# A gated mix of two long convolutions: B's results multiplied by u as they leave PSUM, two holds copied whole, and a new order

## The chip, the cores and the metric

The kernel runs on one core of a Trainium2 chip. Its engines are called PE (TensorE), DVE (VectorE), ACT (ScalarE), POOL (GpSimd) and SP (SyncE). The metric is the device time of one execution in microseconds. The times of before are three runs.

## The reference

For an input u of 2048 steps by 448 channels, two long convolutions along the steps are computed and mixed by a gate:

```python
x = A_u
g = sigmoid((x * gate_w).sum(-1, keepdims=True))
a = A_ref(x, ...)                  # K[d,l] = Re sum_n C * exp(dt*A*l) * dt*B over 256 modes; y = conv(K, u) + u * Dskip
b = B_ref(x, B_k, B_v, ...)        # kv = shift(k) * v over 4 taps; y = conv(ssm_k, kv) + kv * ssm_D; b = x * y
return g * a + (1 - g) * b
```

So B's convolution result is multiplied by u (`q * y` with q = u), and that product is one of the two operands of the gate. Both convolutions are causal and as long as the sequence.

## The kernel before

The 448 channels are four groups of 112. A tile has 128 partitions, made of 4 channel groups times 32 positions, and 64 blocks of 28 channels in its free dimension. The 112 channels of a group are worked on in four heads H of 28 (NC = 28).

A convolution (`conv_B`, `conv_A`) has these steps for each head. `spread_in` is a first short transform by matmuls with Wc and copies to SBUF (`spread`). `transform` is a second one with the table W2, 64 matmuls and eight copies of 128x896. `swapped` makes a copy with the halves of the partitions exchanged, by eight DMAs on SP's or POOL's queue. `products` are two wide multiplications on DVE. `stage_a` transforms back with copies of up to 128x512, and `stage_b` (heads worked on alone) or `stage_b_both` (B of one head and A of the head before, together) ends it. A's kernel is built beforehand by `table(H)`: exponentials and sines on ACT, then `tables`, a chain of products and additions on DVE (three of them with an accumulating DMA on POOL's queue, `split`), then `sums`, 448 small matmuls on PE, and `gather`.

PSUM is four rooms of two banks (`ps0` to `ps3`, `Places.room`); SBUF scratch is eight slots (`q0` to `q7`). The last part of head 3 is `end`, which also stores the rows to HBM over the queues of SP and ACT; `mix(H)` joins a and b for heads 0 to 2.

`PLAN` (line 37) gives the logical order of the work: T is a table, B and b are B's convolutions, a and A are A's, m is a mix. Nothing is issued in this order. Every engine call is recorded in a list (`Listed`, line 120), and `Order.issue` (line 140) issues the calls in the order written out in the string `ORDER` (line 51), with a dependency that keeps each engine to it. All instructions therefore have one line in the profile, 145. Three more strings fix what could be chosen: `SLOTS` (line 38) and `ROOMS` (line 41) give the buffer of each use, and `SIDES` (line 45) says for each call of a `Sides` helper (line 346: `evac`, `evac.turned`, `evac.ahead`, `evac.minus`, `evac.masked`, `evac.queue`) whether it goes to DVE ("V") or ACT ("S"); for `queue` the two letters are POOL's and SP's DMA queue.

The change touches two places. In `Modes.run` (line 718) the real and imaginary parts of A are copied from PSUM into the tiles that hold them for the tables: one for head 0, one for head 1, one for heads 2 and 3, and each in two halves. In `epilogue_B` (line 948) B's results are copied from PSUM to `ug[H]`, the head's part of the tile natv; after the last block of the head one wide DVE product multiplies all 64 blocks by u (`uu`, the tile natu). Head 0 comes through `stage_b` in two rooms of 32 blocks; heads 1, 2 and 3 come through `stage_b_both` in four rooms of 16 blocks each, with A's results of the head before in the same rooms:

```python
        both = pt[:, :, 0:448].rearrange("p h (b t c) -> p h b t c", t=2, c=NC)
        for t in range(2):
            consume[t](b0, 16, both[:, :, :, t])
```

A's side of a room (t = 1) is read by `gated`, a DVE product with the gate. `less(H)` is the term with which PE subtracts the finished `ug[H]` from A's sums.

Of the kernel before, what the change touches and what calls it, by code (L numbers as in the profile page):

```python
# [10 lines left out]
ALU = mybir.AluOpType  # L11
# [27 lines left out]
    "60254113451327565066707216435622473722641555230367571061240"  # L39
)  # L40
ROOMS = (
    "303201320132221133023000100332000020101102013331223132233010132231223133020313021221212111021000320232120101311331120231"
    "31230230312202203230211002013123100022133320222302200321202302202333012331301212103331312131332201202032310"
)
SIDES = (
    "SSSSVVSVVVVSVVSVVVVVVVVVSVVVSSVVVSSSSSVSVVSSVVSVVSVSSVVSVVVVVVVSSSSSSSSSSSSSSSSSVVVSVSSSVSSSSSSSSSSSSSSSSVSSSSVSVSSSSSSS"
    "SSSSSSSSSSSSSVSSVSSSSSSSSSSVSSSSSSSSSSSSSSSSSSVVSVSSSSSSSSSSSSSSSSSVVVVVVVVVSVVSVVVSSSSSSVSSSSSSSSSSSSVVSVSSSSSSSSSSVSVV"
    "SSSSSSSSSSSVSSSVVSSSSSSSSSSSVSSSSVVVVVVVVSVVVVSVVVSSSVSVVSSSSSSSSSSVVVSVVSSSSSSSSSSSSSSVSSSSSVSSSSSSVSSVSVSSVSSSSVSVVSSS"
    "VSSSSVSSVVVVSSSSSSSSSSVVVSSSSVSSSSVSSSVVSS"
)  # L50
ORDER = (
# [650 lines left out]
class Modes:  # L702
# [15 lines left out]
    def run(self):  # L718
        nc, V, evac = self.nc, self.nc.vector, self.evac
        for c, nm in enumerate(("A_re", "A_im")):  # L720
            pt = self.stepped(nm)
            for h0, h1, t in self.hold:
                for f in range(2):
                    evac(t[:, :, c].rearrange("p h (q w) -> p q h w", w=NC)[:, 4 * f:4 * f + 4],
                         pt[:, f, 0:448].rearrange("p (g h w) -> p g h w", g=4, w=NC)[:, :, h0:h1])
# [401 lines left out]
```

## Time and profile before

| what | us |
|---|---|
| median of three runs (lowest, highest) | 249.13 (248.91, 250.43) |
| profiled execution: time | 247.59 |
| profiled execution: span | 245.7 |
| DVE busy, in 399 instructions | 231.3 |
| ACT busy, in 335 | 219.0 |
| PE busy, in 5451 matmuls | 209.4 |
| POOL busy, in 109 | 37.5 |

The profile is of one execution. The span runs from its first instruction to its end; the execution's own time is 1.9 us longer. Busy time counts each instant of an engine once, while the mean of a group is the full duration of one instruction; neighbours overlap a little. In a row of a group, what follows the first bar is busy time and mean in ns, and after the second bar stands the idle time of the engine just before it and what ended it.

### The profile page before, as it was taken

Reading aid. Unit: us, or ns where it says so; the run is one execution under the profiler, and the core shown is the slowest. Engines: PE = TensorE matmul, PEld = TensorE weight load, DVE = VectorE, ACT = ScalarE, POOL = GpSimd, SP = SyncE. Lnnn points to the kernel's source line nnn. Section 1 sums busy time; section 2 is a strip of 40 time slices with the busy share of each in tenths; the row PEclk is TensorE's granted clock in tenths of the full one; section 3 lists DMA queues with packets and bytes.
Section 4 is the critical chain, followed back from the end, with each engine's and each line's share of the span. In section 5 each row is a group of like instructions: output and inputs, shape, how many; then the busy total and the mean of one; then the engine's idle time right before and its main releaser. Section 6 shows DMA issues by size and latency. Waiting matters only on the chain.

```text
span 245.7 us, 12199 instructions
## 1 busy us (share of the span) xinstructions
PE 209.4 (85%) x5451; PEld 185.2 (75%) x5451; DVE 231.3 (94%) x399; ACT 219.0 (89%) x335; POOL 37.5 (15%) x109
## 2 busy tenths in 40 slices
PE   1557688888989999888999977999999999999970
PEld 1445256766979899788998866889999998998850
DVE  6999999999888999999999999999999999999980
ACT  3897999989999999999999999999999998657820
POOL 8600003040000014000002320000134220300000
PEclk9999799999999999999999999999999999999996
DMA  6999599999002189300476593000248720230046
GB/s 140 311 191 147 123 190 229 188 204 167 7 5 64 39 197 205 93 4 5 78 114 122 104 226 100 7 3 5 39 80 152 187 80 5 63 95 3 3 105 197
DMA packets 43443, 26.27 MB, mean 107 GB/s; under 512 B 34144, under 2 KB 40400, under 8 KB 43392
## 3 DMA queue, kind: packets, MB, share of 16 engines
q1 hardware_dynamic: 39088, 15.98, 30.6%
q0 software_dynamic: 3456, 8.60, 17.6%
q10 hardware_dynamic: 848, 0.92, 1.3%
q8 instruction: 42, 0.69, 1.1%
q14 instruction: 9, 0.07, 0.1%
HBM read 9.78 MB, written 2.87 MB: 51 GB/s over the span
## 4 chain that ended last, share of the span: by engine, by line
DVE 34%; ACT 32%; PE 21%; issue 6%; DMA 5%; DVEq 0%; ACTq 0%
PE ps L145 21%; ACT q L145 21%; DVE TQ L145 10%; DVE TP L145 9%; DVE q L145 6%; ACT G L145 4%; DVE natv L145 3%; DMA TP<-TP 2%; ACT ET L145 2%; ACT s_W L145 1%; DMA RK<-in_A_log_dt_dram 1%; DVE RK L145 1%; ACT RK L145 1%; DMA out_dram<-q 1%; DVE ET L145 1%
## 5 line engine op out<-in xcount | busy, mean ns | idle before, releaser
L145 ACT CAST q<-ps 128x896 bf16<-128x896 f32 (+3 forms) x168 | 131.6, 909 | 6.6 <-PE ps L145 6.4
L145 PEld LDWEIGHTS <-G 128*128 128x128 bf16 (+2 forms) x1136 | 35.5, 103 | 15.0 <-issue 6.0
L145 DVE TENSOR_TENSOR TQ<-TQ,ET 128x896 bf16<-128x896 bf16 (+2 forms) x70 | 45.9, 683 | 0.1
L145 PEld LDWEIGHTS <-q 128*128 128x128 bf16 (+2 forms) x784 | 41.0, 134 | 6.3 <-issue 3.5
L145 PE MATMUL ps<-q,s_W 128*128 128x112 bf16 (+1 forms) x544 | 32.6, 210 | 4.5 <-ACT q L145 2.3
L145 PE MATMUL ps<-TP,TQ 128*32 128x32 bf16 x1792 | 32.7, 240 | 2.8 <-DVE TQ L145 1.7
L145 PE MATMUL ps<-sa_R,q 128*128 128x128 bf16 x448 | 33.0, 229 | 1.5 <-issue 1.0
L145 DVE TENSOR_TENSOR q<-q,q 128x3584 bf16<-128x3584 bf16 (+1 forms) x22 | 32.3, 1510 | 1.2 <-ACT q L145 0.9
L145 PEld LDWEIGHTS <-s_W 128*128 128x128 bf16 x544 | 27.6, 97 | 7.6 <-issue 5.5
L145 PEld LDWEIGHTS <-TQ 128*32 128x32 bf16 x1792 | 29.6, 153 | 4.9 <-DVE TQ L145 1.9
L145 DVE TENSOR_TENSOR TP<-TP,ET 128x1792 bf16<-128x1792 bf16 (+3 forms) x25 | 31.7, 1270 | 0.6 <-DMA TP<-TP 0.5
L145 ACT ACTIVATE q<-hold 128x224 bf16<-128x224 f32 (+1 forms) x77 | 28.8, 461 | 0.4 <-DVE hold L145 0.3
L145 POOL DMA_DIRECT2D TP<-TP x15 | 13.4, 958 | 102.3 <-DVE TP L145 33.5
L145 POOL DMA_DIRECT2D q<-q x27 | 15.8, 638 | 57.5 <-DVE q L145 24.4
L145 PEld LDWEIGHTS <-natu 128*64 128x64 bf16 (+1 forms) x288 | 21.0, 208 | 4.6 <-DMA natu<-in_B_k_dram 3.1
L145 PE MATMUL ps<-q,G 128*128 128x56 bf16 (+1 forms) x640 | 20.3, 182 | 0.2 <-ACT q L145 0.2
L145 ACT ACTIVATE ET<-q 128x1344 bf16<-128x1344 int16 (+1 forms) x12 | 17.2, 1456 | 1.1 <-DVE TQ L145 1.0
L145 PE MATMUL ps<-Wc,natu 128*64 128x128 bf16 x224 | 16.0, 285 | 0.2 <-ACT q L145 0.2
L145 PE MATMUL ps<-Wc,natv 128*64 128x128 bf16 x224 | 15.2, 283 | 0.4
L145 PEld LDWEIGHTS <-natv 128*64 128x64 bf16 x224 | 14.7, 212 | 1.1 <-issue 0.2
L145 DVE TENSOR_TENSOR TQ<-TQ 128x448 bf16<-128x448 bf16 (+2 forms) x35 | 15.3, 443 | 0.1
L145 PE MATMUL ps<-G 112*32 112x336 bf16 (+3 forms) x448 | 13.8, 274 | 1.3 <-DVE natv L145 1.1
(97 smaller groups left out, 289.6 us busy)
## 6 DMA issues: line engine op xcount, KB each, us to landing
q<-q SPq DMA_DIRECT2D x37, 112.0 KB, 3.7
TP<-TP POOLq DMA_DIRECT2D x9, 448.0 KB, 5.8
q<-q POOLq DMA_DIRECT2D x27, 112.0 KB, 3.9
natu<-in_B_k_dram SPq DMA_DIRECT2D x2, 896.0 KB, 7.2
natv<-in_B_v_dram SPq DMA_DIRECT2D x8, 224.0 KB, 4.7
q<-in_B_ssm_k_dram SPq DMA_DIRECT2D x16, 112.0 KB, 3.9
natu<-in_A_u_dram SPq DMA_DIRECT2D x8, 224.0 KB, 5.8
TP<-TP POOLq DMA_DIRECT2D x6, 224.0 KB, 4.0
```

The source lines that it names most:

```text
L145: ins = f(*args, **kw)
```

## The change

- `epilogue_B` no longer copies. Each room of B's results is read by a DVE product of the PSUM tile with u's part, which writes `ug[H]` directly. The fourteen copies (two for head 0, twelve for the others), which could go to either engine, and the four wide products are gone; fourteen products from PSUM, all on DVE, stand in their place.
- In `Modes.run`, the tiles that hold one head alone are filled by one copy of both halves: eight copies become four.
- `SLOTS`, `ROOMS`, `SIDES` and `ORDER` are new throughout; `PLAN` is the same. `SIDES` has 384 letters in place of 402, and 112 of them are V in place of 124. The number of recorded calls falls from 6393 to 6385. In the built program DVE has 394 instructions in place of 399; ACT loads a table of functions six times in place of five; of the DMAs, SP's queue has three fewer and POOL's three more.

```diff
 SIDES = (
-    "SSSSVVSVVVVSVVSVVVVVVVVVSVVVSSVVVSSSSSVSVVSSVVSVVSVSSVVSVVVVVVVS...
+    "SSSSVVVSVVVSVVVVVSVVVSVVSVSVVVSSVSVVVVSSVVSVVVVSVVVSSVVVSVVSSSSS...
 )
 ORDER = (
-    "0-1 32 56 155 2 153 156 33 314 225 215 307 7 308-309 319 41 213 4 320 154 218 316 35 214 217 226-227 15 228 38 321 "
+    "0 2 32 218 1 41 176 155 215 303 9 156 33 304 157 153 213 216 305 310 182 38 311 308 214 225 56 312 217 321 219 40 313 "
...
@@ Modes.run
             for h0, h1, t in self.hold:
+                src = pt[:, :, 0:448].rearrange("p f (g h w) -> p f g h w", g=4, w=NC)
+                if h1 - h0 == 1:
+                    evac(t[:, 0, c].rearrange("p (f g w) -> p f g w", f=2, w=NC), src[:, :, :, h0])
+                    continue
                 for f in range(2):
-                    evac(t[:, :, c].rearrange("p h (q w) -> p q h w", w=NC)[:, 4 * f:4 * f + 4],
-                         pt[:, f, 0:448].rearrange("p (g h w) -> p g h w", g=4, w=NC)[:, :, h0:h1])
+                    evac(t[:, :, c].rearrange("p h (q w) -> p q h w", w=NC)[:, 4 * f:4 * f + 4], src[:, f, :, h0:h1])
@@ epilogue_B
         def consume(b0, n, pt):
-            evac(banked(ug[H][:, b0:b0 + n], pt), pt)
-            if b0 + n == 64:
-                V.tensor_tensor(out=ug[H], in0=ug[H], in1=window(uu, 0, 64, H), op=ALU.mult)
+            V.tensor_tensor(out=banked(ug[H][:, b0:b0 + n], pt), in0=pt, in1=banked(window(uu, b0, n, H), pt), op=ALU.mult)
         return consume
```

More of the change, by code (lines that the diff above doesn't have):

```diff
@@ L38 @@
 SLOTS = (
-    "60254113451327565066707216435622473722641555230367571061240"
+    "70207113466365722647545376012373751532706323254561170464230"
 )
 ROOMS = (
-    "303201320132221133023000100332000020101102013331223132233010132231223133020313021221212111021000320232120101311331120231"
-    "31230230312202203230211002013123100022133320222302200321202302202333012331301212103331312131332201202032310"
+    "320100210132032300311322033213101132120311312101203032100021323022200023020313221312211120013012301033112002100210313122"
+    "22211230013230121323231322101332302120113001310230121132333103322020231000231330101023121123102221033312220"
 )
 SIDES = (
[L46 to L49, printed above, removed]
+    "SSSSVVVSVVVSVVVVVSVVVSVVSVSVVVSSVSVVVVSSVVSVVVVSVVVSSVVVSVVSSSSSSSSSSSSSSSSVSSVVSSSSSSSSSSSSSSSSSSSSSSSSSSSSSSSSSSSSSSSS"
+    "SSSSSSVVSVVVSSSSSSSSSSSSSSSSSSSSSSSSSSVSSSVSSSSSSSSSSSSSSVVVVSVSSSVVVSVSVSSSSSSSSSSSSSSSVVVSVSVVSSSSSSSSVSVSSSVVSSSSSSSS"
+    "VVSSSVVSSSSSSSSSSSSSVVVVSVVVVVVSVSVVSSSSVVVSSSSSSSSSVSSSVSSVSSSSSSSSSVSVSSSVSSSVSSSSVSVSSVVSSSSSSSVSSSVVSSVVVSSVSSSVSSSS"
+    "SSSSSSSVVSVSSSSSSSSSVSSS"
 )
 ORDER = (
[60 rows of a table removed]
[59 rows of a table added]
 )
```

117 rows, old and new, of the table ORDER are left out of this document.

## The prediction

> **What bounds the kernel now.** First the first part of the page, then the busy time of each engine in three stretches, then the chain.
>
> ```profile
> span 245.7 us, 12199 instructions
> PE 209.4 (85%) x5451; PEld 185.2 (75%) x5451; DVE 231.3 (94%) x399; ACT 219.0 (89%) x335; POOL 37.5 (15%) x109
> DVE 34%; ACT 32%; PE 21%; issue 6%; DMA 5%; DVEq 0%; ACTq 0%
> ```
>
> DVE is the fullest engine, but the chain is shared almost evenly by three. So no engine's total is the bound; it has to be asked stretch by stretch.
>
> ```profile
> 0.00:60.00 60.00, 41.14 (x736) 30.71 (x737) 57.30 (x135) 52.39 (x81) 14.19 (x72) 0.97 0.96 192
> 60.00:150.00 90.00, 82.72 (x2271) 76.66 (x2268) 86.92 (x112) 89.97 (x137) 11.20 (x17) 1.00 0.44 93
> 150.00:240.00 90.00, 85.30 (x2447) 77.80 (x2447) 87.09 (x154) 76.05 (x119) 12.07 (x20) 1.00 0.26 59
> 240.00:245.70 5.70, 0.19 (x16) 0.03 (x4) 0.00 (x0) 0.54 (x1) 0.00 (x0) 0.62 0.58 190
> ```
>
> The columns after the length are PE, weight load, DVE, ACT, POOL, clock, DMA, GB/s. Up to 60 us DVE leads (57.30 of 60: constants and the first table). From 60 to 150 us ACT has no gap at all (89.97 of 90) and DVE few. From 150 to 240 us ACT has 14 us to spare, while DVE (87.09) and PE (85.30) are both near the end of their means. The last 5.7 us are the store. The pieces of the chain agree:
>
> ```profile
> 105.56 7.04 ACT q L145 x16
> ...
> 214.65 12.17 PE ps L145 x305
> ...
> 226.96 9.17 PE ps L145 x210
> ```
>
> ACT's evacuations carry the middle, PE's matmuls the end.
>
> **Part 1: B's epilogue.**
>
> ```profile
> L145 ACT CAST natv<-ps 128x448 bf16<-128x448 f32 x10 | 6.4, 639 | 1.2 <-PE ps L145 1.1
> L145 ACT CAST natv<-ps 128x896 bf16<-128x896 f32 x2 | 2.3, 1128 | 0.0
> L145 DVE CAST natv<-ps 128x448 bf16<-128x448 f32 x2 | 1.2, 616 | 0.0
> L145 DVE TENSOR_TENSOR natv<-natv,natu 128x1792 bf16<-128x1792 bf16 x7 | 7.4, 1085 | 0.0
> L145 DVE TENSOR_TENSOR natu<-ps,gt 128x448 bf16<-128x448 f32 x12 | 7.3, 617 | 0.0
> L145 DVE TENSOR_TENSOR natv<-ps,natv 128x896 bf16<-128x896 f32 x8 | 8.5, 1081 | 0.0
> ```
>
> Removed: twelve copies on ACT (6.4 + 2.3 = 8.7 us), two on DVE (1.2 us) and four of the seven products over 64 blocks (the other three are the mix; 4 x 1.085 = 4.3 us). Added: fourteen products from PSUM, all on DVE. The trace has both sizes, with another bf16 operand: twelve like the gate's (12 x 0.617 = 7.4) and two like the shift product's (2 x 1.081 = 2.2). DVE gains 7.4 + 2.2 - 1.2 - 4.3 = 4.1 us, ACT loses 8.7. By itself this would feed the fullest engine.
>
> **Part 2: the sides.** The new list answers it. Of the copies in both kernels 32 go from DVE to ACT and 20 come back; the larger ones leave.
>
> ```profile
> L145 DVE CAST q<-ps 128x512 bf16<-128x512 f32 (+4 forms) x16 | 12.2, 786 | 1.6 <-issue 0.8 <-PE ps L145 0.6
> L145 DVE TENSOR_SCALAR q<-hold 128x224 int32<-128x224 f32 x26 | 6.6, 299 | 0.0
> L145 DVE TENSOR_SCALAR q<-q 128x672 int32<-128x672 int32 (+1 forms) x7 | 4.1, 587 | 0.1
> L145 ACT CAST q<-ps 128x896 bf16<-128x896 f32 (+3 forms) x168 | 131.6, 909 | 6.6 <-PE ps L145 6.4
> ```
>
> The bulk: twelve copies into q leave DVE and eight, smaller ones, come (net some 5 us), four net of the 0.299 us steps (1.2) and three net of the 0.587 us ones (1.8). Form by form, with the DVE row for what leaves and the ACT row for what arrives, I estimate -8 us on DVE and +9 on ACT. The holds of A_re and A_im take four copies fewer, but B_re's copy of 896 elements goes to DVE: +1 there, -1.4 on ACT. ACT's list also has six table loads in place of five. Together, with 1.28 us for the load: DVE 4.1 - 8 + 1 = -3 us, ACT -8.7 + 9 - 1.4 + 1.3 = 0. PE has the same matmuls in another order. Durations of neighbours overlap a little, so -3 is the outer value.
>
> **The sixth load** is of the sine set and stands first, ahead of the wait for log_dt:
>
> ```profile
> 1.20 1.28 ACT L145 ACT_TABLE_LOAD   x1 [1.20 <-PEq L1111]
> 4.22 0.21 ACT L145 ACTIVATE TP<-RK 112x4 bf16<-112x4 bf16 x1 [1.74 <-DMA RK<-in_A_log_dt_dram]
> ...
> 111.51 1.08 ACT L145 ACTIVATE q<-q,quarter 128x672 int32<-128x672 int32 x1
> 112.61 1.28 ACT L145 ACT_TABLE_LOAD   x1
> 113.90 2.94 ACT L145 ACTIVATE ET<-q 128x1792 bf16<-128x1792 int16 x2
> ...
> L145 ACT ACTIVATE TP<-TP 128x64 bf16<-128x64 int16 (+1 forms) x3 | 0.9, 305 | 0.2 <-DVE TP L145 0.2
> ```
>
> One load and one small sine, 1.28 + 0.31 = 1.6 us, fit into the 1.74 us wait: I take 0; without that cover 1.3 us late.
> The Trainium skill (ScalarE: Activation LUTs, What ACT_TABLE_LOAD costs) gives a switch of sets 2.66 us, 1.28 for the load and 1.38 for a drain; as an estimate, 2.66 + 0.31 - 1.74 = 1.2 us would then be late, and the sum below 249.0 instead of 247.8. The trace shows no drain: 1.08 + 1.28 us after 111.51 the next step runs. The measurement decides.
>
> **Part 3: up to 150 us.** I took the instructions ahead of each step in both orders. Up to the end of the third table (`tables`, H = 2), which releases its sums on PE, the work ahead is nearly equal: DVE -0.3 us, ACT -0.5 us (an estimate from the same rows). What the new order can remove are gaps:
>
> ```profile
> 4.46 0.17 DVE L145 CAST TP<-TP 112x4 f32<-112x4 bf16 x1 [0.87 <-ACT TP L145]
> 63.18 1.23 DVE L145 CAST q<-ps 128x1024 bf16<-128x1024 f32 x1 [0.65 <-PE ps L145]
> 72.78 3.96 DVE L145 TENSOR_TENSOR q<-q,q 128x3584 bf16<-128x3584 bf16 x2 [0.89 <-ACT q L145]
> 77.58 0.30 DVE L145 COPY TP<-ET 128x448 bf16<-128x448 bf16 x1 [0.84 <-PE ps L145]
> 21.66 0.34 ACT L145 COPY q<-ps 128x224 f32<-128x224 f32 x1 [1.52 <-DVE q L145]
> ...
> 150.63 1.20 PE L145 MATMUL ps<-TP,TQ 128*32 128x32 bf16 x64 [0.77 <-DVE TP L145]
> ```
>
> The last row is the release: the third table's sums, waiting for DVE's TP. Of the gaps, the first: about 0.8 us more of constants now stands ahead of the copy that waits 0.87 us. The spread's copy with the 0.65 us wait goes to ACT. The 1.52 us wait of ACT falls away, since that copy into a held table now comes before the DVE subtraction into the same tile, not behind it; what is late next is that subtraction, which has other work behind it. The two waits at 72 and 77 us stay, being for ACT's last copy of a transform and PE's sums. So DVE can be 0.3 + 0.8 + 0.65 = 1.8 us earlier, ACT 0.5 + 1.5 = 2.0; between 60 and 150 us both are needed, so the smaller counts, 1.8. Other waits must appear in a list whose every stretch is shuffled: bounds 0 (all return elsewhere) and 3.5 (the 0.89 and 0.84 go too). I take 1.8, for the three are named.
>
> **Part 4: 150 to 240 us.** PE's 85.30 us stay, with 4.7 us of gaps. DVE loses some 2 of the 3 us here, but its 87.09 does not set the end alone: the chain's last long pieces are PE's. I take 0. Bounds: -2 (DVE decides after all) and +4.9 (third rival). The swap copies change queues, SP and POOL having three issues fewer and three more; a table's add on POOL's queue now stands behind up to four swaps, some 0.64 us each,
>
> ```profile
> L145 POOL DMA_DIRECT2D q<-q x27 | 15.8, 638 | 57.5 <-DVE q L145 24.4 <-ACT q L145 16.0 <-ACT RK L145 14.6
> ```
>
> that is 2.6 us at most, and in the new order some 10 us of DVE's work lie between the product and the reader of the sum: 0.
>
> **Part 5: the end.**
>
> ```profile
> 239.81 0.38 PE L145 MATMUL ps<-RK,minus 128*32 128x112 bf16 x16 [1.76 <-DVE RK L145]
> 240.24 0.54 ACT L145 ACTIVATE q<-ps 128x448 bf16<-128x448 f32 x1 [4.12 <-DMA out_dram<-q]
> 240.81 0.86 ACTq L145 DMA_DIRECT2D out_dram<-q  x2
> ```
>
> Two stores per queue follow the last copy. In the new order the last copy is on DVE, and three stores per queue (two of its own, one of the copy before) are left: one issue more, 0.86 / 2 = 0.4 us, and DVE's slower copy, 0.1. I take +0.5; bounds 0 and +0.9.
>
> **Sum.** -1.8 + 0 + 0.5 = -1.3 us. The profiled execution took 247.59 us (245.7 of span, 1.9 around it), so 246.3 on its scale. The runs have a median of 249.13 (248.91 to 250.43), 1.5 above it; on the median 247.8.
>
> **The rivals.**
>
> 1. *DVE decides throughout.* All 3 us of load come off, and so do the two gaps taken above: -3.0 - 1.5 + 0.5 = -4.0, 245.1 us. For it: 94% busy and the largest share of the chain. Against it: ACT's 89.97 of 90 with an unchanged load, and PE's end.
>
> 2. *The change doesn't reach the time.* The load of ACT and PE is what it was, and the removed waits come back one step later: 0 + 0.5, 249.6 us. For it: work ahead of the third table within 0.5 us. Against it: the waits have definite causes, and these go.
>
> 3. *The rooms stay full: slower.* In `stage_b_both` a room was read by ACT (B) and DVE (A); now DVE reads it twice, behind whatever stands in its queue.
>
> ```profile
> 223.79 0.26 PE L145 MATMUL ps<-natv,minus 128*128 128x224 bf16 x1
> ...
> 224.81 0.26 PE L145 MATMUL ps<-natv,minus 128*128 128x224 bf16 x1
> ...
> 228.00 1.15 DVE L145 TENSOR_TENSOR natu<-ps,gt 128x448 bf16<-128x448 f32 x2
> ```
>
> PE fills two halves, one room, in 1.02 us (223.79 to 224.81); two such reads take DVE 1.15. There are four rooms in all, and eight such fillings in the stretch where PE is near its end (heads 2 and 3 of B). If each holds PE up by one read, 8 x 0.617 = 4.9 us on top of the sum: 252.7. It begins to decide at three fillings (1.9 us, more than the 1.3 won) and passes 1% at seven. Against it: PE has other work between the fillings, and the whole-head product that followed the last room is gone.
>
> **How the numbers follow.** About 1%, 2.5 us, is what a measurement of this kernel can tell from no change. The forecast, 247.8 with its own range of 246.4 to 249.0, has 0.40; the first rival 0.23; the second 0.19; the third 0.18. Faster by over 1% (below 246.6): the first and a little of the forecast's lower edge, 0.28. Slower by over 1% (above 251.6): the third and a tail of the second, 0.20. Within: 0.52. The range goes from 244.6, just below the first rival, to 252.0, short of the third's full price.
>
> **What would show it.** Right: DVE's busy time 228 to 230 us and ACT's 218 to 220; no wait of over 1 us of ACT near 21 us; the third table's sums on PE begin 1 to 2 us before 150.6 us; PE still over 84 us busy in its last 90. Wrong: sums no earlier (the waits came back); or PE waiting on DVE's natv or natu for over 2 us in all after 150 us (the rooms); or a time below 245.5 (DVE decided).

## The result and the profile after

The changed kernel takes 247.94 us (median of 20 runs, 246.28 to 251.04), the kernel before 249.24 us (20 runs beside them, 247.83 to 250.74). Two of the changed kernel's runs (250.45 and 251.04) were in a slower state and are left out of the ratio. The ratio is 0.9944, 95% interval 0.9923 to 0.9964: 1.4 us or 0.6% less, a small gain that is clear of zero. The forecast was 247.8.

The profiled execution of the changed kernel took 248.35 us, 0.4 above its median; that of the kernel before, 247.59, was 1.65 below its own. So the two spans (246.4 and 245.7 us) run against the medians and may not be subtracted. First the head of the new page, then the stretches of the new kernel (columns as before).

```profile
span 246.4 us, 12201 instructions
PE 209.4 (85%) x5451; PEld 185.5 (75%) x5451; DVE 228.4 (93%) x394; ACT 220.4 (89%) x333; POOL 39.9 (16%) x112
PE 36%; DVE 23%; ACT 19%; DMA 7%; issue 7%; SPq 4%; POOL 0%; DVEq 0%; ACTq 0%; POOLq 0%
```

```profile
0.00:60.00 60.00, 41.10 (x752) 31.18 (x754) 58.41 (x131) 54.48 (x83) 14.64 (x71) 0.97 0.98 190
60.00:150.00 90.00, 82.28 (x2264) 76.23 (x2262) 85.06 (x109) 89.72 (x137) 14.28 (x23) 1.00 0.46 95
150.00:240.00 90.00, 86.05 (x2439) 78.04 (x2439) 84.68 (x156) 76.19 (x115) 10.98 (x18) 0.99 0.25 57
240.00:246.40 6.40, 0.00 (x0) 0.00 (x0) 0.26 (x1) 0.00 (x0) 0.00 (x0) 0.50 0.60 189
```

DVE has 2.9 us less (231.3 to 228.4), ACT 1.4 more. Between 60 and 150 us ACT is as full as it was (89.72 of 90), and DVE's share fell from 86.92 to 85.06: what DVE saved stands there as waiting. The new products cost what the prediction had taken for them (groups by form, busy time and mean):

```profile
L144 DVE TENSOR_TENSOR natv<-ps,natu 128x448 bf16<-128x448 f32 x12 | 7.4, 618 | 0.7 <-PE ps L144 0.6
L144 DVE TENSOR_TENSOR natv<-natv,natu 128x1792 bf16<-128x1792 bf16 x3 | 3.2, 1089 | 0.0
L144 DVE TENSOR_TENSOR natv<-ps,natu 128x896 bf16<-128x896 f32 x2 | 2.2, 1082 | 0.0
```

The row that the prediction had used as the release of the second half, the third table's sums on PE:

```profile
150.26 1.28 PE L144 MATMUL ps<-TP,TQ 128*32 128x32 bf16 x64 [0.26 <-ACT q L144]
```

It starts 0.37 us earlier than in the first trace of before, and another engine releases it. Before, DVE was last (0.77 us); now it is ACT, with an evacuation of a transform that PE runs just ahead of the sums. DVE's last product of the table is ready almost at the same moment:

```profile
148.12 2.02 DVE L144 TENSOR_TENSOR TP<-TP,RK 128x3584 bf16<-128x3584 bf16 x1
```

148.12 + 2.02 = 150.14. DVE and ACT arrive together; had ACT alone been earlier, DVE would have held the sums to within 0.1 us of where they are.

### The profile page after: what moved, and what is told of

Same layout as the page of the kernel before. It is cut to its first block, busy times and chain, and to the rows that moved or that the text cites. A ratio compares the mean times of both kernels' runs of the same rounds, so it can differ in the third digit from the quotient of the medians.

```text
span 246.4 us, 12201 instructions
## 1 busy us (share of the span) xinstructions
PE 209.4 (85%) x5451; PEld 185.5 (75%) x5451; DVE 228.4 (93%) x394; ACT 220.4 (89%) x333; POOL 39.9 (16%) x112
## 4 chain that ended last, share of the span: by engine, by line
PE 36%; DVE 23%; ACT 19%; DMA 7%; issue 7%; SPq 4%; POOL 0%; DVEq 0%; ACTq 0%; POOLq 0%
PE ps L144 36%; ACT q L144 15%; DVE TP L144 10%; DVE TQ L144 5%; SPq L144 4%; DVE q L144 4%; ACT G L144 3%; DMA natu<-in_A_u_dram 3%; DMA gw<-in_gate_w_dram 2%; DMA TP<-TP 2%; DMA q<-in_B_ssm_k_dram 1%; DVE RK L144 1%; DVE ET L144 1%; DVE G L144 1%; DVE natv L144 1%
## 5 line engine op out<-in xcount | busy, mean ns | idle before, releaser
L144 ACT CAST q<-ps 128x896 bf16<-128x896 f32 (+4 forms) x172 | 133.2, 900 | 11.1 <-PE ps L144 10.6
L144 DVE TENSOR_TENSOR TQ<-TQ,ET 128x896 bf16<-128x896 bf16 (+2 forms) x70 | 45.4, 682 | 0.1
L144 PE MATMUL ps<-q,s_W 128*128 128x112 bf16 (+1 forms) x544 | 33.5, 210 | 3.8 <-ACT q L144 2.1
L144 PE MATMUL ps<-sa_R,q 128*128 128x128 bf16 x448 | 33.6, 229 | 3.3 <-issue 1.7
L144 PEld LDWEIGHTS <-natu 128*64 128x64 bf16 (+1 forms) x288 | 21.5, 206 | 4.8 <-DMA natu<-in_B_k_dram 3.6
L144 PE MATMUL ps<-Wc,natu 128*64 128x128 bf16 x224 | 16.5, 284 | 0.5 <-ACT q L144 0.5
L144 PE MATMUL ps<-Wc,natv 128*64 128x128 bf16 x224 | 16.1, 285 | 0.6 <-ACT q L144 0.6
L144 PEld LDWEIGHTS <-natv 128*64 128x64 bf16 x224 | 15.2, 213 | 1.5 <-issue 1.0
```

Source lines behind the costliest of these rows:

```text
L144: ins = f(*args, **kw)
```

## The experiments

Ratios are to the kernel before, run on the same chip in the same rounds, with the 95% interval in brackets; "against the changed kernel" means divided by 0.9944, which is good to about 0.3%, 0.7 us. Each trace is one execution.

**The epilogue alone.** In the kernel before, with its order and its other sides:

```
-            evac(banked(ug[H][:, b0:b0 + n], pt), pt)
-            if b0 + n == 64:
-                V.tensor_tensor(out=ug[H], in0=ug[H], in1=window(uu, 0, 64, H), op=ALU.mult)
+            V.tensor_tensor(out=banked(ug[H][:, b0:b0 + n], pt), in0=pt, in1=banked(window(uu, b0, n, H), pt), op=ALU.mult)
```

> The kernel before with the new epilogue of B alone: its fourteen copies out of PSUM and four of its wide products become fourteen products from PSUM on DVE, at the copies' places in the old order, all other sides as before. By the rows of before DVE gets 4.1 us more (2.5 of them before 150 us), ACT 8.7 less. If both DVE and ACT are needed in the middle and PE at the end (the prediction), the 2.5 us show and the rest mostly not: 250.5 to 252 us against 249.2. If DVE decides throughout: 253.3. If ACT alone decides in the middle: 247 to 248.5.

Measured: 256.6 us, ratio 1.0279 (1.0228 to 1.0330), 7.0 us slower. The page's busy line, the release row, and the two rows of PE's waits for B's and A's results:

```profile
PE 211.0 (83%) x5451; PEld 186.0 (73%) x5451; DVE 234.9 (92%) x407; ACT 214.7 (84%) x323; POOL 37.4 (15%) x109
```

```profile
155.87 1.21 PE L153 MATMUL ps<-TP,TQ 128*32 128x32 bf16 x64 [1.32 <-DVE TP L153]
```

```profile
PE ps L153 <- DVE natu L153: 4.8, 8, 1.0
PE ps L153 <- DVE natv L153: 4.4, 6, 1.8
```

DVE's work grew by 3.6 us, but the sums come 5.2 us later than in the first trace of before, and wait for DVE. That is more than all three cases allowed. PE waits 9.2 us in all for DVE's reads of the rooms (2.7 in the kernel before), 2.0 of it behind 150 us. This is the mechanism of the third rival, in another place.

**The sides alone.** The same kernel with only the engine of 52 copies changed to the new list (32 to ACT, 20 to DVE):

```
-SIDES = (old letters)
+SIDES = (new letters for the copies that both kernels have; B's copies and the holds as before)
```

> The kernel before with the new sides of the 52 copies alone: 32 go from DVE to ACT, 20 from ACT to DVE, at their old places; old epilogue, old order. From the run with the sides undone DVE gets some 6 us less, ACT 5 more. If ACT is needed in the middle, where it had no gap: 3 to 6 us slower than the kernel before, 252 to 255, so that neither the epilogue nor the sides gain anything without the other. If DVE decides throughout: 3 to 6 us faster, 243 to 246.

Measured: 257.65 us, 1.0309 (1.0272 to 1.0346), 7.7 us slower, which is more than the 3 to 6 us of the first case.

```profile
PE 213.8 (84%) x5451; PEld 188.0 (73%) x5451; DVE 225.5 (88%) x387; ACT 225.8 (88%) x347; POOL 37.4 (15%) x109
```

```profile
155.90 1.28 PE L145 MATMUL ps<-TP,TQ 128*32 128x32 bf16 x64 [0.26 <-ACT q L145]
```

DVE has 5.8 us less to do and the kernel is slower all the same, with ACT as the releaser. The two halves of the change each delay the same row by 5.2 and 5.3 us, one through DVE and one through ACT; together they bring it 0.4 us forward. A rival has to be named here: PE's clock. Between 60 and 150 us the granted clock was 0.96 in the trace of the epilogue alone and 0.92 in that of the sides alone, against 1.00 in the first trace of before, so a part of the two delays may be the clock's. It doesn't explain the times: executions of the sides alone whose clock was 0.965 to 0.968 over the whole run took 256.7 to 257.7 us, and those of the kernel before beside them at 0.967 to 0.968 took 249.1 to 249.7.

**The epilogue undone, the sides undone.** In the changed kernel, its order kept: first the old copies at the products' places, the wide product behind the last of each head; then, in a second kernel, the old letters for the 52 copies.

```
-            V.tensor_tensor(out=banked(ug[H][:, b0:b0 + n], pt), in0=pt, in1=banked(window(uu, b0, n, H), pt), op=ALU.mult)
+            copy = V.tensor_copy if (H, b0) in ((2, 48), (3, 32)) else nc.scalar.copy
+            copy(banked(ug[H][:, b0:b0 + n], pt), pt)
```

> The changed kernel with the old epilogue of B: copies (twelve on ACT, two on DVE) at the places of the products, and the wide product behind the last of each head; the new order and sides stay. ACT gets 8.7 us more (4.8 of them before 150 us), DVE 4.1 less. If ACT is full in the middle (89.7 of 90 us), as the prediction has it: 251 to 252.7 us against 247.9 of the changed kernel. If DVE decides throughout: 244 to 246. If neither reaches the time: 247.9 to 249.2.

Measured: 256.19 us, 1.0249 (1.0207 to 1.0291), 7.6 us slower than the changed kernel, which is more than all three cases allowed.

```profile
PE 216.8 (85%) x5451; PEld 189.9 (75%) x5451; DVE 226.3 (89%) x386; ACT 226.8 (89%) x345; POOL 39.9 (16%) x112
```

```profile
153.06 1.28 PE L152 MATMUL ps<-TP,TQ 128*32 128x32 bf16 x64 [0.26 <-ACT q L152]
```

> The changed kernel with the old sides of the 52 copies that both kernels have and that changed engine: 32 go back to DVE, 20 to ACT; the epilogue from PSUM and the new order stay. By the prediction's estimate DVE gets 8 us more, ACT 9 less. If the new sides are what pays for the epilogue: 4 to 8 us slower than the changed kernel, 252 to 256, much like the epilogue alone (256.6). If the order alone pays for it and the sides hardly count: 247.9 to 249.

Measured: 253.8 us, 1.0217 (1.0177 to 1.0256), 6.8 us slower than the changed kernel, as in the first case. DVE is the releaser again:

```profile
PE 211.5 (84%) x5451; PEld 186.1 (74%) x5451; DVE 234.7 (93%) x406; ACT 215.1 (85%) x321; POOL 39.8 (16%) x112
```

```profile
152.13 1.22 PE L144 MATMUL ps<-TP,TQ 128*32 128x32 bf16 x64 [0.75 <-DVE TP L144]
```

Of the 7.6 us that the old epilogue costs, 2.8 have come when the sums start at 153.06 in place of 150.26; the rest comes behind, where ACT has time to spare. DVE's list of waits, in the kernel with the old epilogue, points to how it comes: DVE's products now stand behind single copies of ACT, for 10.7 us in all and 6.0 of it behind 150 us.

```profile
DVE natv L152 <- ACT natv L152: 5.4, 3, 2.8
DVE natu L152 <- ACT natv L152: 5.3, 5, 1.9
```

In all four of these kernels the order was made for other sides or another epilogue, so they show what the parts are worth to each other, not what an order made for them would give.

**One load more, in four places.** Twelve idle copies (128x192 float32, onto themselves) in the changed kernel, two at each of six places:

```
+    for k in (six places of one engine):
+        V.tensor_copy(gx[:], gx[:])          # or nc.scalar.copy
+        nc.extra[k] = 2 * [nc.calls.pop()]   # issued twice behind call k
```

> The changed kernel with twelve idle copies of 128x192 float32 more on DVE, two each at 86, 96, 106, 118, 128 and 138 us, some 0.25 to 0.35 us each, 3 to 4 us in all; nothing needs their result. The changed kernel has 85.1 of 90 us of DVE busy between 60 and 150 us. If DVE and ACT are both needed there (the prediction): 2 to 4 us slower than the changed kernel, 250 to 252. If DVE decides throughout: all of it, 3 to 4 us. If ACT alone decides: under 1 us.

> The same twelve copies on ACT at the same times; ACT has 89.7 of 90 us busy there. If both are needed: 2 to 4 us slower than the changed kernel. If DVE decides throughout: under 1 us. If ACT alone decides: all of it, 3 to 4 us.

> The twelve copies on DVE at 160, 170, 180, 190, 200 and 210 us, where DVE has 84.7 and PE 86.1 of 90 us busy. If PE sets the end there (the prediction's part 4): 0 to 1.5 us slower than the changed kernel. If DVE decides throughout: 3 to 4 us slower.

> The twelve copies on ACT at 160 to 210 us, where ACT has 76.2 of 90 us busy. All theories of the prediction expect under 1 us. If PE waits for ACT's single copies rather than for its total there (a room is not free before its copy has ended), 1 to 3 us.

The busy lines in that order, to be compared with 228.4 and 220.4:

```profile
PE 208.5 (84%) x5451; PEld 185.6 (75%) x5451; DVE 230.8 (94%) x406; ACT 221.0 (90%) x333; POOL 40.0 (16%) x112
```

```profile
PE 211.6 (85%) x5451; PEld 186.6 (75%) x5451; DVE 229.0 (91%) x394; ACT 224.1 (90%) x345; POOL 39.9 (16%) x112
```

```profile
PE 209.4 (85%) x5451; PEld 185.4 (75%) x5451; DVE 230.9 (93%) x406; ACT 220.4 (89%) x333; POOL 39.9 (16%) x112
```

```profile
PE 209.1 (84%) x5451; PEld 185.4 (75%) x5451; DVE 228.5 (92%) x394; ACT 223.7 (90%) x345; POOL 39.9 (16%) x112
```

| place | load added | ratio (interval) | against the changed kernel |
|---|---|---|---|
| DVE, 86 to 138 us | 2.4 us | 1.0036 (1.0014 to 1.0058) | +2.3 us |
| ACT, 86 to 138 us | 3.7 us | 1.0103 (1.0076 to 1.0130) | +4.0 us |
| DVE, 160 to 210 us | 2.5 us | 1.0018 (0.9997 to 1.0040) | +1.8 us |
| ACT, 160 to 210 us | 3.3 us | 1.0039 (1.0012 to 1.0065) | +2.4 us |

On DVE the load came out below the 3 to 4 us expected. In the middle the whole load of either engine shows, within the 0.7 us: both are needed, and neither "DVE decides throughout" nor "ACT alone" holds. The release rows say the same:

```profile
154.41 1.28 PE L152 MATMUL ps<-TP,TQ 128*32 128x32 bf16 x64 [0.26 <-ACT q L152]
```

```profile
151.18 1.19 PE L152 MATMUL ps<-TP,TQ 128*32 128x32 bf16 x64 [0.74 <-DVE TP L152]
```

In both traces the granted clock was 1.00 between 60 and 150 us. With ACT's load the sums come 4.2 us later; with DVE's they come 0.9 later, in an execution 1.4 us below its median, and DVE is the releaser again. The surprise is the last row of the table: ACT, with 14 us of gaps between 150 and 240 us, passes on some 2.4 of 3.3 us, as the case of the single copies had it. DVE's late load, 1.8 of 2.5, lies between its two cases.

**The kernel before once more,** for a second trace, nothing changed.

> The kernel before once more, for a second trace. The third table's sums on PE began at 150.6 us in the first trace, whose execution was 1.6 us faster than the median; in five traces with the new order they began at 150.0 to 150.9. If the gaps removed ahead of them are worth 1.8 us (the prediction's part 3), they begin at 151.5 to 152.5 in an execution near the median. If the waits came back (the second rival): 150.0 to 150.9, and what is won lies behind them.

This execution took 249.41 us, 0.2 above its median.

```profile
151.25 1.20 PE L145 MATMUL ps<-TP,TQ 128*32 128x32 bf16 x64 [0.40 <-DVE TP L145]
```

With 150.63 that makes 150.94 on average. In the six traces with the new order unaltered up to there (the changed kernel, the two late loads and the three tries at the end, below) the sums begin at 150.26, 150.09, 150.24, 150.25, 150.09 and 150.89: 150.30. So 0.6 us is won ahead of the sums, a third of the 1.8, where the two traces of before differ by 0.6 and the six by 0.8; neither expectation fits well.

**The end.** Three tries, all in the changed kernel. First the order of the last two blocks as before (two stores per queue behind the last copy):

```
-... 6195 6364-6379 6328 6196-6211 6380 6212 6381-6382 6216 6213 6215 6214 6383-6384
+... 6195 6327-6328 6196-6211 6270-6271 6212 6362 6214-6216 6363 6272 6364-6379 6213 6380-6382 6384 6383 6269
```

> The changed kernel with the order of its last two blocks as before: one block's copy and most of its stores go out ahead of the last block's steps, so that two stores per queue follow the last copy in place of three or four. From the end of the last matmul to the end of the span the profile of before has 5.5 us, that of the changed kernel 6.8. If the queues' issues set this (0.75 us each), the kernel gets 0.6 to 1.3 us faster than the changed one: 246.6 to 247.3. If the prediction's term of 0.5 us is right: 247.4. If the difference of the two profiles is chance or the data's transfer: 247.9.

Measured: 248.86 us, 0.9962 (0.9938 to 0.9986): no gain over the changed kernel, against which it is 0.4 us slower. Two stores per queue do follow the last copy, but that copy, on ACT, stands behind the stores which ACT itself issues:

```profile
236.72 5.91 SPq L151 DMA_DIRECT2D out_dram<-q  x8
...
237.18 3.43 ACTq L151 DMA_DIRECT2D out_dram<-q  x5
...
239.40 0.38 PE L151 MATMUL ps<-RK,minus 128*32 128x112 bf16 x16 [1.69 <-DVE RK L151]
240.66 0.54 ACT L151 ACTIVATE q<-ps 128x448 bf16<-128x448 f32 x1 [2.96 <-DMA out_dram<-q]
```

Then the stores merged in pairs, 64 rows each (simplified: which of the old stores are kept is left out):

```
-    dmae[x % 2].dma_start(out_rows[x][:, y0:y0 + 4], lines[h][32 * x:32 * x + 32, 4 * k:4 * k + 4])      # x = 0..3
+    dmae[p].dma_start(out_rows[2 * p:2 * p + 2, :, y0:y0 + 4], lines[h][64 * p:64 * p + 64, 4 * k:4 * k + 4])   # p = 0, 1
```

> The changed kernel with its sixteen stores of the end merged in pairs, eight stores of 64 rows, one per queue and block. If an issue costs about the same whatever it moves, the ACT queue's four last issues (3.0 us) become two and the kernel gets 1 to 1.5 us faster: 246.4 to 246.9. If an issue costs by its rows: 247.7 to 247.9.

Measured: 279.71 us, 1.1183 (1.1137 to 1.1229), 32 us slower, which no theory had. The rates from 236 us on in 40 equal slices of the stretch, then the middle of it as a stretch, then the stores of the changed kernel (columns as before; the last three are clock, DMA and GB/s):

```profile
GB/s 0 7 24 24 24 31 45 49 49 56 49 52 52 56 49 52 52 56 49 52 52 56 49 56 49 56 49 52 52 56 49 56 49 56 49 52 52 52 14 0
```

```profile
240.00:275.00 35.00, 0.00 (x0) 0.00 (x0) 0.03 (x1) 0.00 (x0) 0.00 (x0) 0.50 0.13 50
```

```profile
238.00:244.50 6.50, 0.86 (x32) 0.58 (x32) 1.56 (x4) 0.54 (x1) 0.00 (x0) 0.58 0.88 273
```

The same bytes move at some 50 GB/s, against 273 in the changed kernel, and 0.13 of the core's 16 DMA engines is busy, which is two engines' worth, against 0.88. The Trainium skill (DMA: Bandwidth & Descriptors, Why a DMA increments its semaphore by 16 and not by 1) says that a transfer is spread over the largest number of engines, up to 16, that divides the slowest dimension of both its sides; here that became 2, the pair, in place of 32 rows. The trace agrees with it, with the 0.13.

Last, the blocks in the old order, with the first one's copy on ACT, the last one's on DVE and three stores on POOL's queue:

```
+    if h == k:
+        evac.force = "SV"[h]
+    queue = nc.gpsimd if x == 3 and (h, k) != (1, 1) else dmae[x % 2]
```

> The changed kernel with the last two blocks one behind the other as in the kernel before, but with the first one's copy on ACT and the last one's on DVE, and one store in four of the first three blocks on POOL's queue, so that ACT has few stores to issue behind which a copy could wait, and DVE no copy ahead of its last two steps. If the stores' issues and the copy behind them set the last 6 us: 1 to 2 us faster than the changed kernel, 246 to 247. If the landing of the data sets it: 247.5 to 248.

Measured: 249.19 us, 0.9989 (0.9963 to 1.0015), 1.1 us slower than the changed kernel and outside both cases. No version here beats the changed kernel.

## Why the prediction was right, and where only its sum was

**What bounds the kernel: right for the middle.** The two loads added in the middle and the two halves of the change show DVE and ACT both needed up to 150 us. Of the signs that the prediction had named, most came: DVE 228.4 us, no wait of ACT near 21 us, PE 86.05 us busy between 150 and 240; ACT, 220.4, is just above its 218 to 220. The sign of part 3, sums 1 to 2 us before 150.6, did not come: they begin at 150.26.

**The loads (parts 1 and 2): DVE right, ACT not.** DVE fell by 2.9 us (-3 forecast) and ACT rose by 1.4 (0 forecast). The parts behind it were smaller than worked out: the epilogue alone is +3.6 on DVE (4.1) and -4.3 on ACT (-8.7), the sides -5.8 and +6.8 (-8 and +9). So a copy's mean duration overstates what its removal takes off ACT's busy time: the twelve had 8.7 us by their durations, and 4.3 went. The likely reason is that neighbours in a full stream overlap; no run isolates it.

**The sixth load: nearly right.** It is 0.4 us late in place of 0, because the small sine itself waits for DVE:

```profile
1.19 1.28 ACT L144 ACT_TABLE_LOAD   x1 [1.19 <-PEq L1111]
3.06 0.26 ACT L144 ACTIVATE TP<-TP 128x64 bf16<-128x64 int16 x1 [0.59 <-DVE TP L144]
3.34 1.28 ACT L144 ACT_TABLE_LOAD   x1
4.63 0.20 ACT L144 ACTIVATE TP<-RK 112x4 bf16<-112x4 bf16 x1
```

The step that took 4.22 starts at 4.63. The load begins 0.02 us behind the sine and is followed at once: no drain of 1.38 us, as the Trainium skill (ScalarE: Activation LUTs, What ACT_TABLE_LOAD costs) would have it, is to be seen.

**Part 3: the step that failed.** It said "DVE can be 0.3 + 0.8 + 0.65 = 1.8 us earlier", ACT 2.0, "so the smaller counts, 1.8"; 0.6 came. The three named waits did go. But between 60 and 80 us DVE now waits in new places; the rows of the changed kernel, then that stretch before and after:

```profile
67.28 1.63 DVE L144 TENSOR_TENSOR ET<-ET,q 128x1344 bf16<-128x1344 bf16 x2 [1.94 <-ACT q L144]
70.54 0.86 DVE L144 TENSOR_TENSOR ET<-ET,q 128x1344 bf16<-128x1344 bf16 x1 [0.83 <-ACT q L144]
77.31 0.28 DVE L144 COPY TP<-ET 128x448 bf16<-128x448 bf16 x1 [2.02 <-PE ps L144]
```

```profile
60.00:80.00 20.00, 19.33 (x640) 17.97 (x641) 17.62 (x21) 20.00 (x31) 0.52 (x1) 1.00 0.13 31
```

```profile
60.00:80.00 20.00, 19.05 (x623) 17.86 (x623) 15.22 (x21) 20.00 (x33) 1.55 (x3) 1.00 0.17 39
```

ACT was at 20.00 of 20 and PE at 19.3 there already. Now the whole way to the end of the table's last product, which DVE reaches at 150.57 us before and at 150.13 after:

```profile
0.00:150.57 150.57, 123.86 (x3004) 107.37 (x3004) 144.79 (x247) 142.93 (x218) 25.40 (x89) 0.99 0.65 132
```

```profile
0.00:150.13 150.13, 123.38 (x3012) 107.41 (x3012) 143.60 (x240) 144.33 (x220) 28.92 (x94) 0.99 0.67 133
```

DVE's work ahead of the sums fell by 1.2 us, where the step had 0.3. Its waits went from 5.8 to 6.5 us (6.4 in the second trace of before), where the step took 1.45 off. So what came earlier came by work that left DVE, and the term that failed is the gaps: removed in three places, they were back in others. On ACT, up to 150 us, work grew from 142.4 to 144.2 us and the waits fell from 7.6 to 5.8; 1.5 of the 1.8 is the sixth load with its sine, which stand where ACT had waited 1.74 us for log_dt.

**Part 4: 0 came, but the reason given does not hold.** From the sums' start to the end of the last matmul it is 89.6 and 90.2 us in the two traces of before and 89.3 after, though DVE has 2.4 us less to do between 150 and 240 us. ACT's spare time was taken for cover, and DVE's end for harmless. The late loads speak against both: some 0.7 of each added microsecond shows (give or take 0.3), though PE is at 86 of 90, and in their traces the same stretch is 90.6 us with DVE's load and 90.7 with ACT's. The order keeps each engine to its list, so a late copy can hold up whatever follows it, however many gaps the engine has elsewhere; what it held up here is open.

**Part 5: the wrong mechanism.** The step took the last copy and the stores behind it to set the end, +0.5. In the changed kernel and in the two traces of before (the last row being of the second):

```profile
236.91 5.15 SPq L144 DMA_DIRECT2D out_dram<-q  x8
238.73 0.86 PE L144 MATMUL ps<-RK,minus 128*32 128x112 bf16 x32 [1.14 <-DVE RK L144]
```

```profile
236.15 6.12 SPq L145 DMA_DIRECT2D out_dram<-q  x8
```

```profile
237.44 6.94 SPq L145 DMA_DIRECT2D out_dram<-q  x8
...
241.10 0.38 PE L145 MATMUL ps<-RK,minus 128*32 128x112 bf16 x16 [1.76 <-DVE RK L145]
```

From the last matmul's end to the end of the span it is 5.5 and 6.1 us before and 6.8 after: the changed kernel's earlier last matmul bought nothing. From the first store to the end it is 9.5 and 10.2 before, 9.5 after, 9.8 with the old order of blocks; over thirteen traces (all but that of the merged stores) the second distance lies between 9.2 and 10.2 us, the first between 5.5 and 7.8. While the stores run, 0.88 of the DMA engines is busy (the stretch from 238 to 244.5 us above). So the transfer of the sixteen stores looks like the limit, not their last issue. This fits the traces; a kernel that only moves the first store was not run.

**The rivals.** DVE throughout (245.1): refuted by ACT's load in the middle and by the sides alone. Not reaching the time (249.6): half true, for on DVE the waits did come back one step later, but DVE's work ahead of the sums fell by 1.2 us, which this rival left out. The rooms (252.7): after 150 us PE's list of waits in the changed kernel has no row for natv or natu; the mechanism is real, as the epilogue alone shows, and the new sides and order keep it out.

**What stays open.** The sum was -1.3 and -1.4 came, but of its terms -1.8 came as -0.6, and +0.5 rests on a mechanism that the traces don't bear out, so the hit is luck in good part. Of two executions near their medians (249.41 and 248.35 us) the spans differ by 1.2 us, 1.0 of it ahead of the third table's sums; over all traces only 0.6 lies there. Between 60 and 65 us the granted clock was 0.70 in the second trace of before and 1.00 in the first, and by 64 us the second is 1.0 us behind it: DVE waits 1.69 us for PE there in place of 0.65. Single executions vary by as much as what is sought, and the rest can't be placed.

## What to carry to other kernels

When two engines arrive at a stage together, a change that moves work between them can't be priced part by part: here the halves cost 7.0 and 7.7 us alone, in an order not made for them, and gain 1.4 together. Ask which engine releases the stage's first instruction, before and after, and price the change by how far that moves, not by the fullest engine's total. And gaps of an engine that keeps to a list aren't simply room for more work: test a suspected bound by adding a known load at a known place.

## What was not expected of the hardware

- Two stores merged into one, with the pair as the outermost dimension, fell from 273 to some 50 GB/s and cost 32 us.
- ACT's copies wait behind ACT's own stores: the last one 2.96 us behind five issues of 3.43 us.
- With three late stores on POOL's queue the span ended 7.8 us behind the last matmul, the longest of those thirteen, and nothing in the trace says what it waits for.
